# Seven block products for eight in the spatial product of an attention, MoE and gMLP kernel

## The chip, the cores and the metric

The kernel runs on one core of a Trainium2 chip. The metric is the device time of one execution in microseconds. The engines are TensorE (PE, with its weight loads shown as PEld), VectorE (DVE), ScalarE (ACT), GpSimd (POOL) and SyncE (SP), which here issues all transfers.

## What is computed

Three layers follow each other over 4 batches of 1088 tokens: a linear attention, a channel mix (the "MoE" layer) and a gated MLP with a spatial product. The change lies in the last one. Cut to what matters:

```python
def _moe2_ref(x, w_in, w_spatial, b_spatial, w_out):
    h = np.maximum(x @ w_in, 0.0)
    u, v = h[..., :512], h[..., 512:]
    v_n = (v - mean(v)) / np.sqrt(var(v) + 1e-06)
    v_s = np.einsum('ts,bsd->btd', w_spatial, v_n) + b_spatial[None, :, None]
    return ((u * v_s) @ w_out)
```

The spatial product takes, for each batch, the 1088 x 1088 matrix `w_spatial` times the normalised v of 1088 tokens x 512 features. All is float32. To hold precision at TensorE's fast rate, each operand is split into a high and a low part (H and L, `float32r`), and a product is three matmuls: L*H, H*H, H*L (`mm3`, L109 to 112).

## The kernel before

Tokens stand in three chunks `CH` of 384, 384 and 320 target tokens (c = 0, 1, 2). Source tokens stand in eight blocks of 128 (k = 0 to 7) and a tail of 64. The 512 features of v stand in four blocks of 128 (d = 0 to 3).

The first part (up to about 185 us) runs attention and the channel mix for all batches. Its plan gives each piece of work a step g (`plan`, `todo`); in it the weights of the spatial product are loaded and split (`wstep`, `wload`, `wconv`, L410 to 429), and four units of batch 0's gated MLP are put in early.

The second part goes over the batches. A unit is one pair (d, c): `spatial` (L487) makes the up-projection u of its feature block into bank 3 (`mm3`, then a relu by ScalarE, L503), adds eight blocks times three matmuls into one accumulator bank (L506), adds two tail matmuls with the bias (L511, L512), multiplies u by the accumulator on VectorE (L516), and splits that product (copy on ScalarE L519, subtract on VectorE L520). The product with `w_out` is left to a closure (`tail`, L522) that a later unit runs after its fourth block (`gout`, L507); on the fourth feature block its bank is copied and stored (L526, L527). A unit is so 24 + 2 + 3 + 3 = 32 matmuls, 12 units a batch. The very last unit ends in `finish` (L531): two halves on VectorE, each followed by a float32 matmul, a copy and the store.

The v of batch b+1 is made during batch b: `v_tile` (L444) does three matmuls of 512 columns into banks 6 and 7, a relu (L450), mean and variance on VectorE (L454, L455), the inverse root on GpSimd (L456, L457) and the scaling on VectorE (L458), into the tile `VR`, which stays in SBUF. `normalise` (L463) splits it per feature block: copies of 128x512 on ScalarE, subtracts on GpSimd (`low`, L118), and the tail's operands T1 and T2.

SBUF tiles have one buffer per tag and PSUM has eight banks with a tag each, so a new tile of a tag waits until the old one has been read. The order of the instructions on each engine is not the order of the text: a scheduler lays it out when the program is built, with modelled times (`schedule_with_timeline_sim=True`, L815).

Of the kernel before, what the change touches and what calls it, by code (L numbers as in the profile page):

```python
# [8 lines left out]
F32 = mybir.dt.float32  # L9
# [3 lines left out]
ALU = mybir.AluOpType  # L13
# [45 lines left out]
W1G = 69  # L59
W1N = 8  # L60
ORD0 = ((0, 0), (1, 0), (0, 1), (1, 1), (2, 0), (3, 0), (2, 1), (3, 1), (0, 2), (1, 2), (2, 2), (3, 2))
R0 = (1, 5)
R1 = 5
VW = NH * (HD + 1)


@with_exitstack
def attn_moe_gmlp(ctx: ExitStack, tc: tile.TileContext, qT, kT, va, st, wk, wv, wr, win, wout,
# [3 lines left out]

    pool = ctx.enter_context(tc.tile_pool(name="sb", bufs=1))
    pp = ctx.enter_context(tc.tile_pool(name="ps", bufs=1, space=PSUM))

    uid = [0]

# [15 lines left out]
    def m(i):  # L93
        return f"m{i}"
# [11 lines left out]
    ebias = sb("ebias", [128, 1])  # L106
    warm = sb("warm", [128, 1])

    def mm3(out_ap, lH, lL, rH, rL, first, last, late=1):  # L109
        parts = [(lL, rH), (lH, rH), (lH, rL)]  # L110
        for n, (l, r) in enumerate(parts if late else parts[::-1]):
            TE.matmul(out_ap, lhsT=l, rhs=r, start=first and n == 0, stop=last and n == 2)  # L112

    def copy(dst, src):
        return SE.activation(out=dst, in_=src, func=AF.Copy)  # L115
# [274 lines left out]
            VE.tensor_tensor(out=xTs[b][:, o:o + n], in0=vvs.pop(i), in1=sgs.pop(i), op=ALU.mult)  # L390


    wt, xsp, vnt = {}, {}, {}

    WTAGS = (8, 9, 10, 11, 12, 13, 14, 15, 16, 17, 0, 1, 2, 3, 4, 5, 6, 7)

# [44 lines left out]
            low(VE, xL[:, S:], x3, xH[:, S:])  # L441
        xsp[b] = (xH, xL)

    def v_tile(b, j):  # L444
        xH, xL = xsp[b]
        v = VR[:, j]
        pv = bank(rot(6, 7))
# [10 lines left out]
        VE.tensor_scalar(out=v, in0=v, scalar1=mv[:, 0:1], scalar2=rs, op0=ALU.subtract, op1=ALU.mult)  # L458

    GRP = {0: ((0, 8),), 1: ((0, 8),), 2: ((0, 3), (3, 3), (6, 2)), 3: ((0, 8),)}  # L460
    TAGS = {0: (("n0H", "n0L"),), 1: (("n1H", "n1L"),), 2: ((m(8), m(9)), (m(10), m(11)), (m(12), m(13))), 3: (("k0", "k1"),)}

    def normalise(b, d):  # L463
        cs = slice(128 * d, 128 * d + 128)
        Hs, Ls = [], []
        for (j0, n), (tH, tL) in zip(GRP[d], TAGS[d]):
            H, L = sb(tH, [128, n, 128], F32R), sb(tL, [128, n, 128], F32R)
            for j in range(0, n, 4):
                e = min(n, j + 4)
# [13 lines left out]
        vnt[b, d] = (Hs, Ls, T1, T2)  # L483

    po, gout, seen = {}, [], {}

    def spatial(b, d, c, fill, early=False):  # L487
# [17 lines left out]
        for k in range(NK):  # L505
            mm3(acc, Hs[k], Ls[k], *wtile(k, c), k == 0, False, 0)  # L506
            if k == 3 and gout:  # L507
                gout.pop()()
# [4 lines left out]
        if (b, rank, c) == (B - 1, ND, NCH - 1):  # L513
            finish(b, d, c, acc, u)
            return
        VE.tensor_tensor(out=u, in0=acc, in1=u, op=ALU.mult)  # L516
        gH = sb("xrH" if early else rot(m(2), m(3)), [128, n], F32R)
        gL = sb("xrL" if early else rot(m(4), m(5)), [128, n], F32R)
        copy(gH, u)  # L519
        low(VE, gL, u, gH)  # L520

        def tail():  # L522
            mm3(po[c], woH[:, ds], woL[:, ds], gH, gL, rank == 1, rank == ND)
            if rank == ND:
# [6 lines left out]
    def finish(b, d, c, acc, u):  # L531
        o, n = CH[c]
        while gout:
            gout.pop()()
        ob = sb(rot(m(6), m(7)), [128, n])
        step = n // 2
        parts = [slice(x, x + step) for x in range(0, n, step)]
        for cs in parts:
            VE.tensor_tensor(out=u[:, cs], in0=acc[:, cs], in1=u[:, cs], op=ALU.mult)
            TE.matmul(po[c][:, cs], lhsT=wo_last, rhs=u[:, cs], start=False, stop=cs is parts[-1])  # L540
        copy(ob, po[c])
        nc.sync.dma_start(out=out[:, b * S + o:b * S + o + n], in_=ob)


    rawS = sb(m(9), [128, 16, 2], I32)
# [180 lines left out]
        for fn in todo.pop(g, ()):  # L726
            fn()
    assert not todo
    wo_last = sb(m(14), [128, 128])
    ds = slice(DG - 128, DG)  # L730
# [4 lines left out]
    for b in range(B):  # L735
        if b + 1 < B:
            xsplit(b + 1)
        order = ORD0 if b == 0 else [divmod(u, NCH) for u in range(ND * NCH)]
        for u, (d, c) in enumerate(order):
            if b == 0 and u < EARLY:  # L740
                continue
            fill = {}

            def add(k, fn, *a):
                fill.setdefault(k, []).append(lambda: fn(*a))

            if b == 0:
                for k in range(WB[u] if u < len(WB) else 0):
                    add(k, wstep)
            elif u == 0:  # L750
                add(0, normalise, b, ND - 1)
            if b + 1 < B:
                vt = {2: (0, 1), 3: (2, 3), 4: (4, 5), 5: (6, 7), 6: (8,) * (b % 2)}.get(u - (VD0 if b == 0 else 0), ())
                for n, j in enumerate(vt):
                    add(2 + 3 * n, v_tile, b + 1, j)
                nd = {NB0: 0, NB0 + 1: 1, NB0 + 2: 2} if b == 0 else {7: 0, 8: 1, 10: 2}
                if u in nd:
                    add(0, normalise, b + 1, nd[u])
            spatial(b, d, c, fill)
    assert wi[0] >= len(worder) and not pending_raw  # L760
    while gout:
        gout.pop()()


_INS = ["qT", "kT", "va", "st", "wk", "wv", "wr", "win", "wout", "wT", "wtail", "btail", "mu", "ident", "msk"]
# [53 lines left out]
```

## Time and profile before

| what | value |
|---|---|
| median of 3 runs | 469.09 us (468.9 to 469.63) |
| the profiled execution's own time | 468.87 us |
| its span in the trace | 467.1 us |
| TensorE busy | 454.6 us, 97% |
| VectorE / ScalarE / GpSimd busy | 50% / 52% / 41% |

The span is what the trace covers; the execution's own time has some 1.8 us around it. A row of a group of instructions names the line, the engine, the operation, what is written and read (tile names without numbers; `p` is a PSUM bank, `w` the weights' tiles, `m` scratch), how often, the busy time and the mean of one. A timeline row has start and duration in us; consecutive equal instructions are merged (x20), and their durations overlap where the engine is pipelined.

### The profile page before, as it was taken

To read this page: it belongs to the slowest core of one execution; us is meant where nothing else is said; L and a number is where in the kernel's file an instruction comes from. 1 tells how busy PE (TensorE), PEld (TensorE's weight loads), DVE (VectorE), ACT (ScalarE), POOL (GpSimd) and SP (SyncE) were. 2 spreads that over 40 slices of the span, in tenths; PEclk is the share of its full clock that TensorE was granted. 3 is DMA by queue.
4 is the path that set the end of the run, shared out by engine and by line. 5 is a ranking of instruction groups with operands and counts; after the bars stand their busy time and mean duration, and the time that the engine had idled before them with its cause. 6 is when DMAs were issued, how large, how long until landed. Compare 5 with 4: busy or idle time off the path is not lost.

```text
span 467.1 us, 7331 instructions
## 1 busy us (share of the span) xinstructions
PE 454.6 (97%) x2757; PEld 432.7 (93%) x2757; DVE 234.4 (50%) x430; ACT 240.6 (52%) x567; POOL 191.7 (41%) x248
## 2 busy tenths in 40 slices
PE   8978999999999998999999999999999999999997
PEld 8967998989998887999999999999999999999996
DVE  4598768768446796337653435521335421212121
ACT  2585768888776987685327423441433441312111
POOL 2566546486544898455217313440213430200000
PEclk9999999999999999999999999999999999999999
DMA  7972100011000110122000000000100000000001
GB/s 221 359 241 93 49 0 2 17 34 52 27 1 1 42 60 20 34 81 64 1 17 18 15 1 1 0 2 0 50 1 1 0 1 17 32 1 0 2 0 48
DMA packets 12227, 18.77 MB, mean 40 GB/s; under 512 B 1760, under 2 KB 10784, under 8 KB 12192
## 3 DMA queue, kind: packets, MB, share of 16 engines
q1 hardware_dynamic: 12192, 18.31, 12.2%
q8 instruction: 21, 0.34, 0.3%
q14 instruction: 14, 0.11, 0.1%
HBM read 16.08 MB, written 2.23 MB: 39 GB/s over the span
## 4 chain that ended last, share of the span: by engine, by line
PE 78%; DVE 8%; POOL 5%; DMA 3%; ACT 2%; issue 2%; SPq 1%; ACTq 0%; POOLq 0%; DVEq 0%
PE p L112 64%; PE p L386 4%; DVE w L118 2%; POOL m L343 2%; PE p L258 2%; PE p L511 2%; PE p L512 2%; PE p L220 2%; DVE w L128 1%; DMA w<-in_wk_dram 1%; PE p L189 1%; DMA w<-in_qT_dram 1%; PE p L241 1%; DVE mx L298 1%; ACT m L340 1%
## 5 line engine op out<-in xcount | busy, mean ns | idle before, releaser
L516 DVE TENSOR_TENSOR m<-p,m 128x384 f32<-128x384 f32 (+1 forms) x43 | 22.9, 533 | 93.2 <-PE p L512 89.0
L112 PE MATMUL p<-m,k 128*128 128x384 f32 (+1 forms) x288 | 65.8, 348 | 2.7 <-POOL k L133 1.6
L503 ACT ACTIVATE m<-p 128x384 f32<-128x384 f32 (+1 forms) x44 | 20.7, 470 | 75.6 <-PE p L112 73.6
L343 POOL TENSOR_TENSOR m<-m 128x384 f32<-128x384 f32 (+1 forms) x48 | 42.9, 898 | 38.2 <-ACT m L340 32.6
L112 PEld LDWEIGHTS p<-m,k 128*128 128x128 f32 x288 | 48.3, 188 | 6.4 <-POOL k L133 1.8
L112 PE MATMUL p<-w,k 128*128 128x384 f32 (+1 forms) x288 | 52.0, 327 | 0.0
L112 PE MATMUL p<-w,m 128*128 128x384 f32 (+1 forms) x288 | 51.7, 327 | 0.0
L112 PE MATMUL p<-w,n1H 128*128 128x384 f32 (+1 forms) x192 | 48.4, 328 | 0.2 <-DVE x L516 0.2
L112 PEld LDWEIGHTS p<-w,m 128*128 128x128 f32 x288 | 48.1, 188 | 0.4
L112 PEld LDWEIGHTS p<-w,k 128*128 128x128 f32 x288 | 48.0, 188 | 0.3
L340 ACT ACTIVATE m<-p 128x384 f32<-128x384 f32 (+1 forms) x96 | 42.5, 471 | 11.0 <-PE p L112 8.3
L112 PE MATMUL p<-w,n0H 128*128 128x384 f32 (+1 forms) x192 | 48.0, 329 | 0.0
L118 DVE TENSOR_TENSOR w<-m,w 128x384 fp32r<-128x384 f32 (+1 forms) x44 | 33.4, 765 | 28.5 <-POOL m L343 17.0
L118 DVE TENSOR_TENSOR m<-m,m 128x384 fp32r<-128x384 f32 (+1 forms) x47 | 28.9, 616 | 35.5 <-ACT m L115 30.0
L456 POOL TENSOR_SCALAR rs<-mv 128x1 f32<-128x1 f32 x34 | 9.4, 277 | 66.6 <-DVE mv L455 64.1
L450 ACT ACTIVATE VR<-p 128x512 f32<-128x512 f32 x34 | 20.3, 601 | 31.2 <-PE p L112 31.1
L112 PEld LDWEIGHTS p<-w,n1H 128*128 128x128 f32 x192 | 34.3, 188 | 1.5 <-DVE x L516 0.5
L112 PEld LDWEIGHTS p<-w,n0H 128*128 128x128 f32 x192 | 34.1, 188 | 0.8
L386 PE MATMUL p<-w,wvT 128*128 128x384 f32 (+1 forms) x88 | 34.3, 471 | 0.0
L112 PE MATMUL p<-w,n0L 128*128 128x384 f32 (+1 forms) x96 | 31.8, 331 | 0.9 <-POOL n0L L118 0.9
L112 PE MATMUL p<-w,n1L 128*128 128x384 f32 (+1 forms) x96 | 31.7, 330 | 0.0
L454 DVE BATCH_NORM_STATS2 bn<-VR 128x6 f32<-128x512 f32 x34 | 23.3, 688 | 13.8 <-ACT VR L450 13.8
(193 smaller groups left out, 1031.2 us busy)
## 6 DMA issues: line engine op xcount, KB each, us to landing
st<-in_wT_dram SPq DMA_DIRECT2D x16, 192.0 KB, 2.4
w<-in_kT_dram SPq DMA_DIRECT2D x8, 192.0 KB, 4.8
w<-in_qT_dram SPq DMA_DIRECT2D x8, 192.0 KB, 4.7
out_dram<-m SPq DMA_DIRECT2D x8, 192.0 KB, 1.9
st<-in_wT_dram SPq DMA_DIRECT2D x8, 160.0 KB, 2.2
xs0H<-in_va_dram SPq DMA_DIRECT2D x2, 528.0 KB, 5.2
xs0L<-in_va_dram SPq DMA_DIRECT2D x2, 528.0 KB, 6.2
w<-in_wk_dram SPq DMA_DIRECT2D x2, 512.0 KB, 6.8
```

The source lines that it names most:

```text
L112: TE.matmul(out_ap, lhsT=l, rhs=r, start=first and n == 0, stop=last and n == 2)
L118: return eng.tensor_tensor(out=L, in0=src, in1=H.bitcast(F32), op=ALU.subtract)
L220: TE.matmul(kv[:, w * g:w * g + w], lhsT=kp, rhs=vt if wide else vt[:, VP * g:VP * g + VP], start=(t == 0), stop=(t == NT - 1))
L258: nd_pe[0] = TE.matmul(o.rearrange("p h c -> p (h c)"), lhsT=qt[g][:, cut(c, t)], rhs=kb[:, g], start=not wide or g == 0, stop=not wide or ...
L340: SE.activation(out=r, in_=hk, func=AF.Relu)
L343: anchor[2] = GE.tensor_tensor(out=sq, in0=r, in1=r, op=ALU.mult)
L386: TE.matmul(vvs[i], lhsT=wvT[:, f // 2], rhs=hls.pop(g), start=f == 0, stop=f == NF - 1)
L450: SE.activation(out=v, in_=pv, func=AF.Relu)
L454: VE.bn_stats(out=bn, in_=v)
L456: GE.tensor_scalar(out=rs, in0=mv[:, 1:2], scalar1=1e-6, scalar2=None, op0=ALU.add)
L503: SE.activation(out=u, in_=pu, func=AF.Relu)
L516: VE.tensor_tensor(out=u, in0=acc, in1=u, op=ALU.mult)
```

## The change

For batches 1 to 3 units are replaced by groups. A group (b, p) takes two feature blocks d = p and e = p + 2, and all three chunks. For chunks 0 and 1 the source blocks are cut into two halves of four. That makes a 2 x 2 block product (features by source halves, source halves by chunks), which Strassen's scheme (in Winograd's form) does in seven products of four blocks each, in place of eight. Chunk 2 is done as before, with eight blocks per output.

The scheme needs sums of blocks on both sides. Sums of the weights (sets 1 to 4 in `ctile`, and the tail's set 5) are made once, during units 4 to 11 of batch 0, from weights loaded again: for each block k of a half, two VectorE operations for sets 1 and 3 and three for sets 2 and 4, and per set a copy on ScalarE and a subtract on GpSimd (table `W2`). Sums of v are made per group by `build`: four VectorE operations of 128x512, and for each of the eight sets a copy of 128x512 on ScalarE and a subtract on GpSimd.

v of batches 1 to 3 no longer stays in `VR`: `v_tile` writes it to DRAM, and `quad_load` reads a quarter (four blocks of one feature block, 512 bytes a row) back for each of the four operands of a group. Banks: 0 is X, 1 is Y, 6 is Z and chunk 2's accumulator, 3 and 7 rotate between up-projections and V tiles, 2, 4 and 5 hold the output products. In chunks 0 and 1 the relu of u is no longer ScalarE's: one VectorE instruction takes the maximum of the bank and zero and multiplies by the joined product (`gated_out`).

Cut to its core:

```diff
+W2 = {4: ((6, "fl", 2),), 5: ((1, "fs", 2), (1, "fl", 3)), 6: ((1, "fs", 3), (2, "fl", 0)),
+      7: ((1, "fs", 0), (2, "fl", 1)), 8: ((1, "fs", 1), (4, "sl", 2), (4, "sl", 0)), 9: ((1, "ss", 2), (4, "ss", 0), (7, "sl", 1)),
+      10: ((4, "ss", 1), (7, "sl", 3)), 11: ((4, "ss", 3),)}
+BUILD = (11, 12, 22, 21, 2, 1, 3, 4)
+RING = ("n1H", "n1L", "k0", "k1")
...
-    def v_tile(b, j):
+    def v_tile(b, j, banks=(6, 7)):
...
+        if b and j < NK:
...
+            nc.sync.dma_start(out=vdram[b][:, j], in_=v)
...
+    def parts(n, k, src):
+        H, L = ctile(n, k)
+        copy(H, src)
+        low(GE, L, src, H)
+
+    def first_sums(k):
+        r11, r12, r22 = raws.pop(k)
+        tt(VE, r11, r12, r11, ALU.subtract)
+        parts(1, k, r11)
+        tt(VE, r22, r22, r12, ALU.subtract)
+        parts(3, k, r22)
...
+    def build(b, p, i):
+        n = BUILD[i]
+        A = {x: quad.get((b, p, x)) for x in (11, 12, 21, 22)}
+        if n == 2:
+            tt(VE, A[22], A[21], A[22], ALU.add)
+            tt(VE, A[21], A[11], A[21], ALU.subtract)
+            tt(VE, A[11], A[22], A[11], ALU.subtract)
+        if n == 4:
+            tt(VE, A[12], A[12], A[11], ALU.subtract)
...
+        copy(t[:, 0], src)
+        low(GE, t[:, 1], src, t[:, 0])
...
+        def gated_out(pu, C, d, c):
+            VE.scalar_tensor_tensor(out=C, in0=pu, scalar=0.0, in1=C, op0=ALU.max, op1=ALU.mult)
+            put_out(b, d, c, C)
...
+        d, e = p, p + 2
+        X = bank(0)[:, :CMAX]
+        prod(X, 11, 11, True)
+        a = snap(X)
+        flush()
+        u = pre(d, 2, True)
+        acc = bank(6)[:, :CH[2][1]]
+        plain(acc, 11, True)
+        flush()
+        yield
+        Y = bank(1)[:, :CMAX]
+        prod(Y, 12, 21, True)
+        tmm(Y, d, wtile(NK, 0))
+        pu = pre(d, 0)
+        gated_out(pu, join(Y, a), d, 0)
+        plain(acc, 12, False)
+        tmm(acc, d, wtile(NK, 2))
+        tt(VE, u, acc, u, ALU.mult)
+        put_out(b, d, 2, u)
+        yield
+        Y = bank(1)[:, :CMAX]
+        prod(Y, 22, 4, True)
...
+        yield
+        prod(X, 2, 2, False)
+        u2 = snap(X)
+        flush()
+        yield
+        Z = bank(6)[:, :CMAX]
+        prod(Z, 1, 1, True)
+        yield
+        prod(X, 3, 3, False)
+        tmm(X, e, wtile(NK, 1))
+        u3 = snap(X)
+        pu = pre(e, 1)
+        c22 = sb(rot(m(8), m(9), m(10), m(11)), [128, CMAX])
+        gated_out(pu, join(Z, u3, c22), e, 1)
+        pu = pre(e, 0)
+        gated_out(pu, join(Y, u3), e, 0)
+        yield
+        prod(Z, 4, 22, False)
+        tmm(Z, d, wtile(NK, 1))
+        if last_group:
+            while gout:
+                flush()
+            pu = pre(d, 1)
+            ob = sb(rot(m(6), m(7)), [128, CMAX])
+            for h in range(2):
+                cs = slice(CMAX // 2 * h, CMAX // 2 * h + CMAX // 2)
+                tt(VE, u2[:, cs], Z[:, cs], u2[:, cs], ALU.add)
+                VE.scalar_tensor_tensor(out=u2[:, cs], in0=pu[:, cs], scalar=0.0, in1=u2[:, cs], op0=ALU.max, op1=ALU.mult)
+                TE.matmul(po[1][:, cs], lhsT=wo_last, rhs=u2[:, cs], start=False, stop=h == 1)
...
+        else:
+            flush()
+            pu = pre(d, 1)
+            gated_out(pu, join(Z, u2), d, 1)
...
+        for st, _ in enumerate(group(b, p)):
+            if st < 4:
+                build(b, p, st + 4)
+            elif nxt:
+                build(*nxt, st - 4)
+            if nxt:
+                if st in (1, 2):
+                    quad_load(*nxt, (11, 12)[st - 1])
+                if st in (3, 4):
+                    quad_load(*nxt, (22, 21)[st - 3])
+                if st in (5, 6):
+                    tails(nxt[0], nxt[1] + 2 * (st - 5), vtail[:, 0])
+            if b + 1 < B:
+                if p == 0:
+                    v_tile(b + 1, st, (3, 7))
+                elif st == 0 and b % 2:
+                    v_tile(b + 1, NK, (3, 7))
```

In it `prod(acc, a, w, first)` is four blocks of `mm3` with v's set a and the weights' set w, `plain` the same with chunk 2's weights, `tmm` the two tail matmuls, `pre` the three matmuls of an up-projection, `snap` ScalarE's copy of a bank to SBUF, `join` a VectorE add of a bank and such a copy, `flush` the next output product that waits, and `put_out` the split of a gated product. `finish` is gone.

## Rows read from the trace of the kernel before

**Rows 1.** The page's head and busy times by engine, whole span.
```profile
span 467.1 us, 7331 instructions
...
PE 454.6 (97%) x2757; PEld 432.7 (93%) x2757; DVE 234.4 (50%) x430; ACT 240.6 (52%) x567; POOL 191.7 (41%) x248
```
**Rows 2.** Busy time per stretch: batch 0's second part, batches 1 to 3.
```profile
core 0: us, PE busy (x) PEld busy (x) DVE busy (x) ACT busy (x) POOL busy (x), PEclk, DMA share, GB/s
215.00:262.00 47.00, 47.00 (x283) 45.95 (x282) 24.32 (x49) 22.89 (x51) 19.03 (x30) 1.00 0.06 18
262.00:462.00 200.00, 200.00 (x1191) 197.74 (x1190) 64.19 (x125) 60.05 (x134) 40.39 (x62) 1.00 0.02 8
```
**Rows 3.** Waits of TensorE from 185 us on, all of them.
```profile
engine line waited for: us in total, times, longest us
PE p L112 <- DVE x L516: 0.2, 1, 0.2
```
**Rows 4.** Timeline of TensorE: 20 matmuls and the next one.
```profile
431.69 3.65 PE L112 MATMUL p<-w,m 128*128 128x384 f32 x20
435.18 0.31 PE L112 MATMUL p<-m,woL 128*128 128x320 f32 x1
```
**Rows 5.** Timeline of the last 5 us, from the last tail matmuls.
```profile
462.10 0.31 PE L511 MATMUL p<-w,T 128*128 128x320 f32 x1
...
462.24 0.31 PE L512 MATMUL p<-w,wrH 128*128 128x320 f32 x1
...
462.59 0.56 DVE L539 TENSOR_TENSOR m<-p,m 128x160 f32<-128x160 f32 x2 [2.29 <-PE p L512]
...
464.33 0.33 SPq L542 DMA_DIRECT2D out_dram<-m  x1
```
**Rows 6.** Timeline: a last matmul and its reader.
```profile
441.90 0.33 PE L512 MATMUL p<-w,T 128*128 128x384 f32 x1
...
442.28 0.56 DVE L516 TENSOR_TENSOR m<-p,m 128x384 f32<-128x384 f32 x1 [3.40 <-PE p L512]
```
**Rows 7.** Instruction groups from 262 to 462 us, other engines.
```profile
L516 DVE TENSOR_TENSOR m<-p,m 128x384 f32<-128x384 f32 (+1 forms) x35 | 18.8, 536 | 85.6 <-PE p L512 81.4 <-ACT m L115 4.1
...
L503 ACT ACTIVATE m<-p 128x384 f32<-128x384 f32 (+1 forms) x36 | 17.0, 472 | 70.3 <-PE p L112 68.3 <-DVE m L516 1.9
...
L454 DVE BATCH_NORM_STATS2 bn<-VR 128x6 f32<-128x512 f32 x17 | 11.8, 692 | 10.0 <-ACT VR L450 10.0
...
L450 ACT ACTIVATE VR<-p 128x512 f32<-128x512 f32 x17 | 10.2, 600 | 22.9 <-PE p L112 22.9
L457 POOL TENSOR_TENSOR rs<-rs,half 128x1 f32<-128x1 f32 x17 | 9.6, 563 | 1.3
L458 DVE TENSOR_SCALAR VR<-VR,mv,rs 128x512 f32<-128x512 f32 x17 | 9.3, 546 | 11.2 <-POOL rs L457 11.2
...
L118 POOL TENSOR_TENSOR n1L<-VR,n1H 128x512 fp32r<-128x512 f32 x4 | 5.2, 1294 | 3.0 <-ACT n1H L115 3.0
...
L115 ACT ACTIVATE n1H<-VR 128x512 fp32r<-128x512 f32 x4 | 2.5, 628 | 1.3 <-PE p L112 1.3
```
**Rows 8.** Timeline of TensorE: output matmuls between two tail matmuls.
```profile
457.26 0.34 PE L511 MATMUL p<-w,T 128*128 128x384 f32 x1
457.44 0.34 PE L112 MATMUL p<-m,woL 128*128 128x384 f32 x1
457.61 0.34 PE L112 MATMUL p<-m,woH 128*128 128x384 f32 x1
457.79 0.34 PE L512 MATMUL p<-w,wrH 128*128 128x384 f32 x1
```
**Rows 9.** Line L118 over the span: duration ns min/median/max.
```profile
L118 DVE TENSOR_TENSOR w<-m,w x44: 478/558/1620, 27.9 to 190.2; 128x384 fp32r<-128x384 f32 x32, 128x320 fp32r<-128x320 f32 x12
L118 POOL TENSOR_TENSOR w<-st,w x15: 877/1015/1338, 89.4 to 217.1; 128x384 fp32r<-128x384 f32 x11, 128x320 fp32r<-128x320 f32 x4
```
**Rows 10.** Transfers by issue: KB each, median us to landing.
```profile
st<-in_wT_dram SPq DMA_DIRECT2D x16, 192.0 KB, 2.4
...
out_dram<-m SPq DMA_DIRECT2D x8, 192.0 KB, 1.9
```
**Rows 11.** Transfer queue: packets, MB, share of 16 engines' time.
```profile
q1 hardware_dynamic: 12192, 18.31, 12.2%
```
**Rows 12.** Timeline of TensorE: the last V tile of batch 1.
```profile
239.02 0.39 PE L112 MATMUL p<-winL,xs1H 128*128 128x512 f32 x1
```

More of the change, by code (lines that the diff above doesn't have):

```diff
@@ L107, in attn_moe_gmlp, with mm3 @@
     warm = sb("warm", [128, 1])
-    def mm3(out_ap, lH, lL, rH, rL, first, last, late=1):
+    def mm3(out_ap, lH, lL, rH, rL, first, last, late=1, skip=False):
         parts = [(lL, rH), (lH, rH), (lH, rL)]
         for n, (l, r) in enumerate(parts if late else parts[::-1]):
-            TE.matmul(out_ap, lhsT=l, rhs=r, start=first and n == 0, stop=last and n == 2)
+            TE.matmul(out_ap, lhsT=l, rhs=r, start=first and n == 0, stop=last and n == 2, skip_group_check=skip)
     def copy(dst, src):
@@ L529, in spatial @@
         gout.append(tail)
[L531 to L542, printed above, removed]
+    ct = {}
@@ new lines, in tt, with stage, first_load @@
+    def tt(eng, o, a, b_, op):
+        return eng.tensor_tensor(out=o, in0=a, in1=b_, op=op)
+    raws = {}
+    def stage(j):
+        return VR[:, j, :CMAX]
+    def first_load(k):
+        raws[k] = [stage(j) for j in rot(*FSET)]
+        for x, n in zip(raws[k], (11, 12, 22)):
+            wraw(x, n, k)
+    def parts(n, k, src):
[8 more added lines that the diff above has]
+        parts(3, k, r22)
@@ new lines, in second_load, with second_sums, tail_sums @@
+    def second_load(k):
+        raws[k] = [stage(j) for j in SSET[k]]
+        for x, n in zip(raws[k], (11, 21)):
+            wraw(x, n, k)
+    def second_sums(k):
+        a, c = raws.pop(k)
+        H, L = [x.bitcast(F32) for x in ctile(3, k)]
+        tt(VE, a, a, H, ALU.add)
+        tt(VE, a, a, L, ALU.add)
+        tt(VE, c, c, a, ALU.subtract)
+        parts(2, k, a)
+        parts(4, k, c)
+    def tail_sums():
+        H, L = ctile(5, NK)
+        x, y = sb(m(10), [128, CMAX]), sb(m(11), [128, CMAX])
+        nc.sync.dma_start(out=x, in_=btail[:, :CMAX])
+        nc.sync.dma_start(out=y, in_=btail[:, CMAX:2 * CMAX])
+        tt(VE, x, x, y, ALU.subtract)
+        parts(5, NK, x)
+        VE.tensor_copy(L[64:65], H[64:65].bitcast(F32))
+        copy(H[64:128], H[0:64].bitcast(F32))
@@ L760, in attn_moe_gmlp, with add @@
-    assert wi[0] >= len(worder) and not pending_raw
+    vtail = sb("wvT", [128, 1, DG])
+    GE.tensor_copy(vtail[:, 0], VR[:, NK])
+    xsplit(1)
+    for u, (d, c) in enumerate(ORD0):
+        if u < EARLY:
+            continue
+        fill = {}
+        def add(k, fn, *a):
+            fill.setdefault(k, []).append(lambda: fn(*a))
+        for k in range(WB[u] if u < len(WB) else 0):
+            add(k, wstep)
+        for n, j in enumerate({4: (0, 1), 5: (2, 3), 6: (4, 5), 7: (6, 7)}.get(u, ())):
+            add(2 + 3 * n, v_tile, 1, j)
+        for k, fn, *a in W2.get(u, ()):
+            add(k, {"fl": first_load, "fs": first_sums, "sl": second_load, "ss": second_sums}[fn], *a)
+        if u == 9:
+            for n in (11, 12):
+                add(2, quad_load, 1, 0, n)
+        if u == 11:
+            for n in (22, 21):
+                add(0, quad_load, 1, 0, n)
+        if u == 10:
+            add(2, tails, 1, 0, vtail[:, 0])
+            add(1, build, 1, 0, 0)
+        if u == 11:
+            add(1, build, 1, 0, 1)
+        spatial(0, d, c, fill)
@@ new lines, in attn_moe_gmlp @@
+    assert wi[0] >= len(worder) and not pending_raw
+    groups = [(b, p) for b in range(1, B) for p in range(2)]
+    for gi, (b, p) in enumerate(groups):
+        nxt = groups[gi + 1] if gi + 1 < len(groups) else None
+        if gi == 0:
+            tail_sums()
+            build(1, 0, 2)
+            tails(1, 2, vtail[:, 0])
+            build(1, 0, 3)
+        if p == 0 and b + 1 < B:
+            xsplit(b + 1)
+        for st, _ in enumerate(group(b, p)):
[10 more added lines that the diff above has]
+                    tails(nxt[0], nxt[1] + 2 * (st - 5), vtail[:, 0])
+            if b + 1 < B:
+                if p == 0:
+                    v_tile(b + 1, st, (3, 7))
+                elif st == 0 and b % 2:
+                    v_tile(b + 1, NK, (3, 7))
```

151 lines of the change are left out of this document (109 added, 42 removed).

## The prediction

> **What bounds the kernel now.** I read the busy shares first [rows 1]: TensorE 97%, the others half or less. A share over the whole span can hide a stage with another limit, so I then took the stretches that the change touches [rows 2]. In batch 0's second part (215 to 262 us) and in batches 1 to 3 (262 to 462 us) TensorE is busy in every microsecond at a granted clock of 1.00 (2.4 GHz), while VectorE, ScalarE and GpSimd are busy 32%, 30% and 20% of the latter. Busy matmuls can overlap and so hide idle time; the view of waits excludes that: after 185 us TensorE waits once, for 0.2 us [rows 3]. So from 185 us to the end the time is the number of matmuls times their spacing. One matmul of 384 columns lasts 0.34 us, but matmuls are pipelined, so that is not their spacing: 20 of them begin at 431.69 and the next matmul at 435.18 [rows 4], which is 3.49 / 20 = 175 ns.
>
> **The products removed: -12.6 us.** Two halves of the eight source-token blocks, two feature blocks (d, d+2) and two chunks of targets took 4 outputs x 8 blocks x 3 = 96 matmuls. Seven half-length products take 7 x 4 x 3 = 84. All other matmuls (the two tail matmuls per output, the up-projections, the output products, chunk 2) keep their number. Twelve fewer in each of 6 groups is 72, all of 384 columns: 72 x 0.175 = 12.6 us. Nothing else fills TensorE here, so all of it is on the path.
> The Trainium skill's page "TensorE: Matmul & The Clock Gate", section "Back-to-back issue gap", gives columns / 2.4 + 2.5 ns for a warm matmul, 162.5 ns here; by it the saving is 11.7 us and the total 0.9 us higher. The trace has 175, and I keep that.
>
> **The end: +0.6 us.** Before, the last two tail matmuls start at 462.10 and 462.24 and VectorE's halves start at 462.59; three output matmuls run beside them; the span ends at 467.1, 4.86 us after 462.24 [rows 1, 5]. The last group instead flushes two output products and makes an up-projection behind its last product: 9 matmuls, 1.58 us, before the gate can read the up-projection. VectorE's first half then starts some 1.95 us after the last tail matmul began in place of 0.35, so the tail is 1.6 us longer; but 9 - 3 = 6 matmuls (1.05 us) of the count have moved into it. Net 0.55 us. The join of the halves runs beside those matmuls and is free; that cover goes if the scheduler puts the flushes earlier, but so does the 0.55.
>
> **Hand-overs of PSUM banks: +3.0 us (0 to 6).** Now every product is 12 matmuls (2.1 us) and products share banks: X is read and added to again, Y and Z as well. I went through each place where TensorE writes a bank that another engine has just read, or needs a weight just built. All but one have a product of 2.1 us or more between; the shortest of these is the output product flushed after product M2 (it needs a multiply, a copy and a subtract, some 2.2 us against 2.6 of cover). The one that is short is Z before its second product: the tail matmul of M3 ends in X, ScalarE copies X out, VectorE adds that to Z, and only then may TensorE add to Z. In rows: 0.38 from the start of a last matmul to its reader (441.90 to 442.28) [rows 6], 0.47 for the copy, 0.56 for the add [rows 7], and 0.1 for two signals, in all 1.51 us. Behind the tail matmul stand two up-projections, 6 matmuls; with its own slot 7 x 0.175 = 1.22 us. So 0.3 us is bare. In two groups (pass 0 of batches 1 and 2) a V tile stands there too, whose bank is held until the gate has read the up-projection, 0.6 us more: 0.9. 4 x 0.3 + 2 x 0.9 = 3.0 us. The low bound is 0: the instruction order is made by a scheduler at build time, and before it puts matmuls of one chain between those of another (two output matmuls between the tail matmuls, 457.26 to 457.79 [rows 8]), so it may put the next group's first product there. The high bound is twice it, 6.0, if a VectorE instruction of 0.5 us stands ahead of the add in each group. I take 3.0, since no row shows this gap filled.
>
> **Other engines in batches 1 to 3: 0.** VectorE gets 24 adds of 128x512 (no row; by 0.56 for 384 columns about 0.75, 18 us) and 24 joins (13.4 us). ScalarE gets 24 more copies of 128x512 at 0.63 and 18 snapshots for 24 activations less, about +12 us; GpSimd 24 more subtracts at 1.29, 31 us [rows 7]. With what they do now, 64, 60 and 40 us of 200 [rows 2], none passes 52% of the 187 us that remain. Each set is built two stages or more (at least 24 matmuls, 4.2 us) before its product; that is the cover.
>
> **Batch 0: +0 (0 to 4).** The sums of weights add 20 VectorE adds (11 us), 16 copies (8 us) and 16 GpSimd subtracts at 1.02 (16 us) [rows 9] to 24, 23 and 19 us of 47 [rows 2]; some 8 us of GpSimd work (batch 1's splits, four of 1.29 us and three shorter ones) moves later, less 2.6 for two new sets. TensorE hides it while each unit's subtract comes within a unit (32 matmuls, 5.6 us). The sums themselves are needed from the fifth stage of the first group, 17 us after batch 0.
>
> **Transfers: 0.** 20 weight blocks, 2 tail rows, 24 writes of V and 24 reads are issued on SP's queue, 70 x 0.33 us [rows 5] over 250 us. Weight loads land in 2.4 us, stores in 1.9 [rows 10]. The reads come in 512-byte pieces, 512 packets; 12,192 packets now take 12.2% of 16 engines' 467 us [rows 11], 75 ns each, so one takes about 512 / 16 x 75 ns = 2.4 us. The chain from the last V tile of batch 1 to a weight is some 10 us (0.6 relu, 1.7 statistics and GpSimd, 0.55 scaling, 1.9 + 2.4 transfers, 1.9 to build, and signals); that tile's matmuls begin at 239.02 [rows 12], and its first use lies past 262. SP's queue holds output stores behind a read that waits for its buffer; nobody waits for those but the output copy two units later.
>
> **Sum.** -12.6 + 0.55 + 3.0 = -9.05. The profiled execution's own time is 468.87, so 459.8; the median of the runs is 0.22 higher, hence **460.0**.
>
> **Rivals.**
> *All covered* (18%): the scheduler fills the bare place, -12.05, 457.0 us; without the tail's cost 456.5. For it: one short wait in 280 us before. Against: the order is laid out with modelled times, and the new chain is serial.
> *The joins queue up* (21%): VectorE works in order, and next to the joins stand statistics (0.69), scaling that waits for GpSimd, and 0.75 us adds. If in each group one such instruction with its wait, 0.9 us, stands ahead of the join, 6 x 0.9 = 5.4 on top: 465.4 us, the case spanning 462 to 468. For it: the fixed order and two more dependent steps; against: VectorE is about half busy.
> *No change* (4%): the hand-overs give back 12.05 / 6 = 2.0 us a group, nearly a whole product; then 469. This is also what the profile would show if the added products were not the ones left out: the matmul count tells.
> *Batch 0 dams up, slower* (7%): VectorE and GpSimd slow each other. The subtract of row L118 takes 558 ns at the median and up to 1,620, GpSimd's 1,015 and up to 1,338 [rows 9]. At a stretched 1.4 and 1.34 us the additions alone are 20 x 1.4 + 16 x 1.34 = 49 us; with GpSimd's other 11 to 14 (19 less 8, and the two sets) and VectorE's other two-input subtracts, a dozen of 0.56, this passes the 47 us by some 20, each unit's subtract waits in that queue, and TensorE with it: about 480 us. It decides against the change where the overrun passes 9 us, that is, where the additions take over 38 us of shared time; at median rates they are 20 x 0.56 + 16 x 1.02 = 27 us.
> The Trainium skill's page "SBUF — State Buffer", section "Who interferes with whom", says that a VectorE instruction with two SBUF inputs and a GpSimd one that reads SBUF exclude each other for a whole instruction; by that the two add up rather than overlap. The long maxima agree with it.
>
> **How the numbers follow.** The forecast has 50%, its own range 458.5 to 462. The range takes in full cover (456.5) and most of the queued joins: 456.5 to 467.5; outside lie no change, slower and a sliver of the third case, some 13%. A measurement of this kernel tells about 0.2%, 0.9 us. Faster 50 + 18 + 21 = 89%, same 4%, slower 7%.
>
> **What would show it.** 72 matmuls fewer and the spacing still 175 ns; TensorE waiting for a VectorE add once a group, 0.3 to 0.9 us, 3 us in all; batch 0's second part no longer than 47 to 48 us; at the end about 6.5 us from the last product's tail matmul to the end. Wrong would be waits of TensorE on GpSimd or DMA in batch 0, waits at more than one place of a group, a changed first part (before 185 us), or a granted clock under 1.00.

## The result and the profile after

The changed kernel takes 471.84 us (median of 11 runs, 470.84 to 474.71), the kernel before 469.09 beside it (11 runs): a ratio of 1.006, 95% interval 1.0043 to 1.0078. It is 0.6% slower; the forecast was 460.0 (456.5 to 467.5). The medians below leave out one execution each of e1, e2 and e5, which ran 5% to 90% longer than the others of the same kernel.

The page's head and busy times of the changed kernel, as [rows 1]:
```profile
span 472.9 us, 7556 instructions
...
PE 447.5 (95%) x2685; PEld 421.6 (89%) x2685; DVE 288.1 (61%) x501; ACT 260.6 (55%) x600; POOL 244.7 (52%) x287
```
72 matmuls are gone (2757 to 2685), as forecast, but TensorE is no longer busy throughout. All of its waits from 185 us on, in place of the single one of [rows 3]:
```profile
PE p L124 <- ACT m L127: 5.8, 5, 2.0
PE p L124 <- DVE m L577: 2.4, 3, 1.2
PE p L124 <- DVE m L130: 1.5, 2, 1.2
PE p L124 <- DVE x L402: 1.4, 1, 1.4
PE p L124 <- ACT m L519: 0.5, 1, 0.5
PE p L124 <- ACT m L352: 0.4, 1, 0.4
PE p L124 <- DVE x L529: 0.2, 1, 0.2
```
To compare stretch by stretch I cut both traces at the same matmuls: the second tail matmul of unit (1, 1), that of batch 0's last unit, and the last one of all. The two middle stretches in the changed kernel, then a part of the first of them:
```profile
core 0: us, PE busy (x) PEld busy (x) DVE busy (x) ACT busy (x) POOL busy (x), PEclk, DMA share, GB/s
215.30:271.26 55.96, 49.59 (x278) 46.57 (x278) 39.31 (x70) 25.80 (x59) 34.60 (x42) 0.97 0.48 151
271.26:466.81 195.55, 190.18 (x1126) 185.60 (x1125) 103.04 (x176) 77.22 (x159) 78.84 (x90) 1.00 0.17 54
256.40:259.80 3.40, 3.40 (x13) 3.40 (x14) 0.83 (x2) 1.18 (x3) 1.60 (x2) 0.51 0.73 199
```
The two stretches before:
```profile
213.83:260.18 46.35, 46.35 (x278) 45.30 (x278) 25.00 (x49) 21.61 (x48) 18.03 (x29) 1.00 0.06 19
260.18:462.24 202.06, 202.06 (x1203) 199.80 (x1202) 64.68 (x126) 61.80 (x138) 41.83 (x63) 1.00 0.02 8
```

| stretch, us | before | after | difference | forecast |
|---|---|---|---|---|
| start to unit (1, 1) | 213.83 | 215.30 | +1.5 | 0 |
| batch 0's second part | 46.35 | 55.96 | +9.6 | 0 (to 4) |
| batches 1 to 3, to the last tail matmul | 202.06 | 195.55 | -6.5 | -10.65 |
| from there to the end | 4.86 | 6.09 | +1.2 | +1.6 |
| span | 467.1 | 472.9 | +5.8 | -9.05 |

(-10.65 is the forecast's -12.6, less 1.05 for the six matmuls that it put into the tail, plus 3.0 for the hand-overs.) Batch 0's second part has the same 278 matmuls and lost most. The profiled execution took 474.71 us, 2.9 over the median, so a usual run loses less than this table shows; the stretch at 0.51 of full clock (256.4 to 259.8 us) is part of it.

**Inside batch 0.** VectorE's timeline there; the columns are start, duration, engine, line, operation, and in brackets the idle time before it and what ended that:
```profile
235.82 0.56 DVE L577 TENSOR_TENSOR VR<-VR,t 128x384 f32<-128x384 f32 x1 [1.85 <-DMA VR<-in_wT_dram]
...
236.90 0.54 DVE L577 TENSOR_TENSOR VR<-VR,t 128x384 f32<-128x384 f32 x1
237.36 0.54 DVE L470 TENSOR_SCALAR VR<-VR,mv,rs 128x512 f32<-128x512 f32 x1
238.18 1.31 DVE L577 TENSOR_TENSOR VR<-VR,x 128x384 f32<-128x384 f32 x1 [0.28 <-DMA VR<-in_wT_dram]
...
239.51 0.52 DVE L529 TENSOR_TENSOR m<-p,m 128x384 f32<-128x384 f32 x1
```
And TensorE's, at the same place:
```profile
237.56 1.04 PE L124 MATMUL p<-w,m 128*128 128x384 f32 x5
240.63 0.44 PE L124 MATMUL p<-m,woL 128*128 128x384 f32 x1 [2.03 <-ACT m L127]
```
The last tail matmul of this unit began at 231.60 us. Its multiply (L529) runs at 239.51, behind three adds of the weight sums (L577): the first waited 1.85 us for a reloaded block, the last 0.28 us and then took 1.31. Copy and output matmul follow the multiply, and TensorE stands 2.0 us. The wait is put down to ScalarE's copy, the last link; the late ones are the adds ahead of the multiply, two links back.

The block is late because SyncE's queue, which issues the reloads (L574), works in order too:
```profile
225.57 0.54 SPq L574 DMA_DIRECT2D VR<-in_wT_dram  x1
231.59 0.33 SPq L474 DMA_DIRECT2D vd<-VR  x1
232.06 2.63 SPq L574 DMA_DIRECT2D VR<-in_wT_dram  x3
```
From 226.1 to 231.6 us it stands at a store of V (L474), whose scaling VectorE finishes only then; three reloads stand behind that store, and the add of 235.82 starts when the first of them has landed. SyncE's waits of this kind from 210 to 272 us are 14.4 us in all:
```profile
SPq L474 <- DVE VR L470: 14.4, 6, 5.4
```
So two queues hold each other up: reloads wait for VectorE's scaling, and VectorE's gate (multiply, and later the subtract) waits behind adds for the reloads. No run issued the reloads ahead of the stores, so what this order alone costs is open.

### The profile page after: what moved, and what is told of

Same layout as the page of the kernel before. It is cut to its first block, busy times and chain, and to the rows that moved or that the text cites. A ratio compares the mean times of both kernels' runs of the same rounds, so it can differ in the third digit from the quotient of the medians.

```text
span 472.9 us, 7556 instructions
## 1 busy us (share of the span) xinstructions
PE 447.5 (95%) x2685; PEld 421.6 (89%) x2685; DVE 288.1 (61%) x501; ACT 260.6 (55%) x600; POOL 244.7 (52%) x287
## 4 chain that ended last, share of the span: by engine, by line
PE 59%; DVE 16%; POOL 10%; DMA 5%; issue 4%; ACT 4%; SPq 1%; POOLq 0%; ACTq 0%; DVEq 0%
PE p L124 47%; DVE VR L470 4%; PE p L398 4%; DVE w L130 2%; DMA VR<-in_wT_dram 2%; POOL m L355 2%; PE p L270 2%; DVE bn L466 2%; POOL rs L469 2%; PE p L232 2%; DMA w<-in_wk_dram 2%; DVE w L140 1%; POOL w L130 1%; PE p L201 1%; DMA w<-in_qT_dram 1%
## 5 line engine op out<-in xcount | busy, mean ns | idle before, releaser
L130 POOL TENSOR_TENSOR k<-VR,k 128x512 fp32r<-128x512 f32 x26 | 33.9, 1305 | 47.4 <-ACT k L127 35.4
L577 DVE TENSOR_TENSOR m<-p,m 128x384 f32<-128x384 f32 (+2 forms) x37 | 19.2, 520 | 61.0 <-PE p L676 34.1
L352 ACT ACTIVATE m<-p 128x384 f32<-128x384 f32 (+1 forms) x96 | 42.4, 470 | 11.1 <-PE p L124 8.3
L127 ACT ACTIVATE m<-m 128x384 fp32r<-128x384 f32 (+2 forms) x45 | 22.7, 504 | 38.1 <-DVE m L689 27.0
L470 DVE TENSOR_SCALAR VR<-VR,mv,rs 128x512 f32<-128x512 f32 x33 | 31.6, 963 | 15.5 <-POOL rs L469 15.2
L127 ACT ACTIVATE k<-VR 128x512 fp32r<-128x512 f32 x26 | 16.2, 629 | 36.5 <-PE p L124 28.4
L124 PEld LDWEIGHTS p<-w,n1L 128*128 128x128 f32 x168 | 29.2, 192 | 0.3
L466 DVE BATCH_NORM_STATS2 bn<-VR 128x6 f32<-128x512 f32 x33 | 22.5, 686 | 11.0 <-ACT VR L462 10.9
L124 PE MATMUL p<-m,woH 128*128 128x384 f32 (+1 forms) x86 | 26.6, 332 | 1.5 <-DVE m L130 1.5
L124 PE MATMUL p<-w,xs1H 128*128 128x384 f32 (+1 forms) x88 | 25.1, 339 | 2.9 <-DVE w L130 2.9
L130 POOL TENSOR_TENSOR n1H<-VR,n1H 128x512 fp32r<-128x512 f32 x12 | 15.5, 1292 | 23.1 <-ACT n1H L127 18.8
```

The costliest lines, as they stand in the source:

```text
L130: return eng.tensor_tensor(out=L, in0=src, in1=H.bitcast(F32), op=ALU.subtract)
L352: SE.activation(out=r, in_=hk, func=AF.Relu)
L577: return eng.tensor_tensor(out=o, in0=a, in1=b_, op=op)
```

## The experiments

Theories. **W**: batch 0's loss is VectorE's queue standing behind adds that wait for late reloads. **C**: it is the added work itself, VectorE and GpSimd slowing each other. **J**: the waits in batches 1 to 3 come from what stands ahead of the join on VectorE, or ahead of the snapshot on ScalarE.

**e1_no_sums**: no reloads and no sums; the products read resident weight blocks, so batches 1 to 3 compute something else.
```
-        if n == 4:
-            return wtile(k, 1)
+        if n in (1, 2, 3, 4):
+            return wtile(*{1: (k, 0), 2: (k + HALF, 1), 3: (k + HALF, 0), 4: (k, 1)}[n])
...
-        for k, fn, *a in W2.get(u, ()):
+        for k, fn, *a in ():
```


> The sums of weights and their reloads are left out; the seven products take plain weights in their place (so sets 1 to 4 are not the scheme's). Everything else stays: 84 products a group, V through DRAM, the same hand-overs. In the changed kernel batch 0's second part ends 9.6 us later than before relative to its start. Theory 1, that the work added to batch 0 is the loss: that part is back within 1 us of the 46.3 us it took before (213.83 to 260.18), and the median falls by 8 to 10 us to some 463 us. Rival, that V's trip through DRAM and the three V slots delay batch 0: the part stays over 50 us and the median over 467.

**e3_reloads_only**: the reloads stay, first_sums and second_sums return at once.

> The 20 reloads are issued as in the change, but no sum is made of them (sets 1 to 4 are plain weights). If the transfers alone were the loss (SP's queue in order, V's stores behind the reloads, V slots), batch 0's second part would stay over 51 us and the median over 467. Theories W and C both say that transfers alone cost little: the part within 2 us of the run without sums and reloads, median 463 to 465.

**e2_sums_of_resident**: the sums stay, made of the high parts of resident blocks; no reloads.
```
-        tt(VE, r11, r12, r11, ALU.subtract)
+        tt(VE, r11, h12, h11, ALU.subtract)
```


> The sums are made by the same VectorE, ScalarE and GpSimd instructions, but from the weights' high parts that lie in SBUF, with no reload (20 transfers of 192 KB less; the low parts are left out of the sums). Theory W, that VectorE's queue stands still at adds whose blocks land late: batch 0's second part falls by 5 us or more, median 465 to 467. Theory C, that VectorE and GpSimd slow each other and the amount of work is the loss: it falls by less than 2.5 us, median over 469.5, and adds beside a GpSimd subtract still take 1.0 us or more instead of 0.56.

Measured: e1 465.12 us (ratio to before 0.9908, 0.9894 to 0.9922), e3 465.17 (0.9914, 0.9902 to 0.9927), e2 468.83 (0.999, 0.9981 to 0.9999). e1 falls by 6.7 us, not by the 8 to 10 that I had taken from the profiled execution. Batch 0's second part is 46.4 us in e1, 46.1 in e3 and 50.2 in e2. The stretch of [rows 2] in e3, then in e2:
```profile
215.00:262.00 47.00, 47.00 (x283) 45.80 (x282) 25.08 (x52) 19.88 (x45) 14.88 (x27) 1.00 0.53 171
```
```profile
215.00:262.00 47.00, 44.43 (x257) 41.90 (x256) 37.75 (x65) 23.73 (x53) 34.60 (x41) 1.00 0.32 103
```
The transfers alone cost nothing, at 171 GB/s in place of 18. The sums alone cost 3.8 us of the part (50.2 against 46.4; 3.7 by the medians of e2 and e1): that is C. What is left needs both, adds that wait for what is reloaded (W): 471.84 - 468.83 = 3.0 us by the medians, 5.8 in the profiled execution, with its stretch at half clock. So neither theory alone is enough: the part falls by what W asked for (5 us or more), the median lies between the two forecasts. The trip of V through memory is in all three and costs nothing in this part.

**e7_no_gpsimd_subtracts**: the sums' 16 GpSimd subtracts become ScalarE copies, so the sums' low parts are other numbers.
```
-        low(GE, L, src, H)
+        copy(L, src)
```


> The changed kernel (its own order) in which the 16 GpSimd subtracts of the weight sums, about 1.0 us each, are 16 ScalarE copies; the low parts of the sums then hold the whole sums, so the output of batches 1 to 3 is not the reference's. It measures what GpSimd's share of the sums costs by itself. Theory C (GpSimd's subtracts slow VectorE's two-input instructions beside them, 3.8 us of the 9.6 that batch 0's second part lost): the part falls from 56 to about 52 us and the time from 471.8 to about 468. Theory W alone (VectorE's adds wait for transfers, and GpSimd has nothing to do with it): within 1 us of the changed kernel. More than 5 us less would say that the waits for transfers arise only because the slowed adds release the staging buffers late.

Measured 469.87 us (1.0009, 0.9998 to 1.0019), second part 49.2 us. VectorE's adds there, and what they waited for:
```profile
L577 DVE TENSOR_TENSOR VR<-VR x11: 541/551/801, 217.4 to 259.0; 128x384 f32<-128x384 f32 x11
...
  DMA VR<-in_wT_dram: 7.8, 7
```
The part is 6.7 us shorter than in the changed kernel's profile, of which 1.7 return behind it; by the medians, which leave out that profile's 2.9 us, the kernel is 2.0 us faster. That lies between the theories: C's 3.8 us are not all GpSimd's. Nor do the shares simply add. In e2, seven adds that read two resident blocks have a median of 1281 ns, beside GpSimd; in the changed kernel, whose adds wait for reloads, the ten of the largest group have 546 ns (both for L577 from 215 to 262 us). e2's 3.7 us is what the sums cost where nothing waits, not a part of the changed kernel's time that can be pointed at. The adds still wait 7.8 us for reloads (4.5 us in the changed kernel in the same window), so these waits don't come from slowed adds that free the staging buffers late.

**e4_order**: in each group the two up-projections go behind X's last tail matmul, and the next group's copies and tails behind the snapshot.
```
-        pu = pre(e, 1)
+        pu = behind([x_last], pre, e, 1)
...
-                build(*nxt, st - 4)
+                behind(snapped if st == 6 else [], build, *nxt, st - 4)
```


> Only the order is changed: the two up-projections are queued behind X's last tail matmul of product M3 (the scheduler had put them ahead of it), and the copies of the next set and tail that ScalarE does there are queued behind the snapshot of X. Theory O, that the hand-over of Z is bare because its cover was moved ahead of it and ScalarE's copies stand before the snapshot: the six gaps of TensorE, 0.8 to 1.3 us each (6.2 in all) fall to 0.3 or less in the four groups without V tiles, 3.5 to 4.5 us, median 467.3 to 468.5. Rival J, that the join waits behind VectorE's scaling: the gaps at M4 of pass 0 of batches 1 and 2 (1.0 and 0.5) stay, and if all are of that kind the median falls by less than 1.5 us.

Measured 466.73 us (0.9946, 0.9932 to 0.996). That is 5.1 us less than the changed kernel, more than the 3.5 to 4.5 that I expected. A hand-over of the changed kernel, with the first matmul of its two up-projections:
```profile
328.23 0.34 PE L124 MATMUL p<-xs1H,winL 128*128 128x384 f32 x1
...
334.07 0.34 PE L676 MATMUL p<-w,wrH 128*128 128x384 f32 x1
...
334.14 0.63 ACT L127 ACTIVATE k<-VR 128x512 fp32r<-128x512 f32 x1 [1.35 <-issue]
334.68 0.29 ACT L127 ACTIVATE T<-wvT 64x128 fp32r<-64x128 f32 x1
...
334.88 0.47 ACT L127 ACTIVATE m<-p 128x384 f32<-128x384 f32 x1
...
335.40 0.79 PE L124 MATMUL p<-w,n1H 128*128 128x384 f32 x3 [0.99 <-ACT m L127]
```
The same place in e4_order:
```profile
331.22 0.34 PE L676 MATMUL p<-w,wrH 128*128 128x384 f32 x1
...
331.39 0.34 PE L124 MATMUL p<-xs1H,winL 128*128 128x384 f32 x1
...
331.59 0.49 ACT L127 ACTIVATE m<-p 128x384 f32<-128x384 f32 x1 [0.43 <-PE p L676]
...
332.44 1.38 PE L124 MATMUL p<-w,n1H 128*128 128x384 f32 x7
```
In the changed kernel the instruction order had put the up-projections 5.8 us ahead of the tail matmul, so nothing stood between it and the next group's first product, which writes the same bank; and the snapshot that frees the bank stood behind a 0.63 us copy for a later product. In e4_order six matmuls cover a snapshot that starts at once. Four waits of 0.8 to 1.2 us are gone; two, of 0.9 and 0.7 us (0.8 and 0.4 in the changed kernel), stay in the groups that also make V tiles. The two halves of the edit were not tried apart.

**e8_join_first** (with e5's edit, below): the scaling of one V tile, and its store, go behind the join.
```
+                    if held:
+                        behind(joined, held.pop())
+                    f = v_tile(b + 1, st, (3, 7), st == 5)
```


> e5_late_weight with one edit in the groups that also make a V tile in every stage: the scaling of the V tile of the sixth stage, and its store, are queued behind the join that reads Z, instead of ahead of it. Theory J (in these two groups the join stands behind a scaling that waits for GpSimd, and TensorE waits 1.0 and 0.9 us at 301.5 and 368.2 us): both waits fall to 0.3 us or less, and the time falls by 1.0 to 1.4 us, to about 464.5. Rival (the join is late because of the chain copy, add, matmul itself; 0.6 us of bank wait): the waits stay above 0.6 us and the time falls by under 0.5 us.

Measured 464.15 us (0.9896, 0.9882 to 0.9909). Both waits are gone; TensorE is busy throughout batches 1 to 3:
```profile
267.54:456.25 188.71, 188.59 (x1126) 185.81 (x1125) 103.05 (x175) 76.94 (x159) 79.54 (x90) 1.00 0.17 56
```
J holds. The gain is larger than the 1.0 to 1.4 us expected: 2.3 to 2.9 us on e5's two runs, and 2.2 us in this stretch (190.86 in e5b). The stretch is 6.8 us shorter than in the changed kernel (195.55), and 13.35 shorter than before: 77 matmuls fewer, which are 81 of 384 columns less and 4 of 320 more, 81 x 0.175 - 4 x 0.147 = 13.6.

**e5_late_weight** and **e5b_late_weight_again** (e4_order and this edit): the sum of the output weights is made in batch 0, not at 162 us.
```
-    GE.tensor_tensor(out=wo_last, ...)
...
+            behind([vt_copy], GE.tensor_tensor, wo_last, ...)
```


> The e4_order kernel with one more edit: the sum woH + woL (the weight of the last two matmuls, one GpSimd add of 0.62 us) is queued on GpSimd behind the copy of V's ninth tile, in batch 0's second part, instead of at build time wherever a buffer is free. In the changed kernel that add stands at 162.1 us between the two GpSimd steps (add, power) that a V tile's scaling waits for. Theory (the add delays the last V tile before the first tail matmul, and the rest of the first part is as before): the first tail matmul of unit (1,1) goes back from 214.6 to about 213.6 to 213.9 us, and the time falls by 0.7 to 1.2 us against e4_order (466.73), to about 465.7. Rival (the first part's extra 1.0 to 1.5 us is scatter from run to run, or comes from the new buffers' places): no change, 466.7.

> e5_late_weight once more, unchanged: it was to be 0.7 to 1.2 us faster than e4_order (466.73) and came out at 467.06, while two kernels that hold its edit (e6 and e8) have their first tail matmul of unit (1,1) at 214.0 us against 214.56 in e4_order. Theory (the edit gives back 0.6 us of the first part, and batch 0's second part took it away again, by 0.5 to 1 us more of waits there): unit (1,1) at 214.0 us, second part 55.5 us or longer, time 466.2 to 467.2. Rival (the edit gains nothing, and 214.0 belongs to the other edits): unit (1,1) at 214.5 or later.

GpSimd's timeline in the changed kernel:
```profile
161.45 0.59 POOL L468 TENSOR_SCALAR rs<-mv 128x1 f32<-128x1 f32 x1
...
162.13 0.62 POOL L953 TENSOR_TENSOR idn<-woH,woL 128x128 f32<-128x128 f32 x1
...
162.71 0.56 POOL L469 TENSOR_TENSOR rs<-rs,half 128x1 f32<-128x1 f32 x1
...
163.30 1.51 DVE L470 TENSOR_SCALAR VR<-VR,mv,rs 128x512 f32<-128x512 f32 x1 [0.87 <-POOL rs L469]
```
Measured 467.06 us (0.995, 0.9937 to 0.9963), and 466.46 again (0.9938, 0.9924 to 0.9951), against 466.73 (0.9946, 0.9932 to 0.996). In e5b's trace unit (1, 1) is at 213.78, as before the change (213.83; e4_order 214.56), and the second part takes 53.9 us (e4_order's profile, which has the half clock, 55.0). That comparison alone is weak, since traces differ by up to 0.9 us from early on: the matmul that begins at 161.69 us before the change, just ahead of this place, begins between 161.43 and 162.29 in the others. Counted from that matmul, unit (1, 1) comes 52.1 us later before the change, 53.1 in each of the six traces with the early add (the changed kernel, e1, e2, e3, e4, e7), and 52.1 to 52.5 in the five with the late one (e5b, e6, e8, e9, e10). So the add costs 1.0 us, and the edit gives back 0.6 to all of it; the other 0.5 us of the table's +1.5 is such scatter, as the rival said. The forecast of a longer second part was wrong; and of the 1.0 us at most a few tenths are left at the end, which is below what the runs can tell.

**e6_sums_behind** (e5 and this edit): the sums' adds go behind the subtract that ends the previous unit's gate (its multiply, copy and subtract).
```
-            add(k, {"fl": first_load, "fs": first_sums, ...}[fn], *a)
+            add(k, (lambda f, a: behind(gls[-1:], f, a)) if fn[1] == "s" else lambda f, a: f(a), f, *a)
```


> e5_late_weight with the weight sums' VectorE adds queued behind the subtract that ends the last unit's gate, so that a unit's multiply and subtract stand ahead of adds that wait for late reloads; everything else as there. Theory W (most of batch 0's extra 9 us is VectorE's queue standing behind adds that wait for transfers): batch 0's second part falls from 55 us to about 50, and the time to 460 to 462 us. Rival C (VectorE and GpSimd slow each other and simply have more to do; the order hardly matters): the part stays above 53 us and the time within 1.5 us of e5_late_weight. Between them, 462 to 464, if the waits only move to the next unit.

Measured 463.92 us (0.9882, 0.9869 to 0.9895):
```profile
214.00:260.13 46.13, 46.13 (x276) 44.97 (x276) 30.52 (x61) 22.37 (x49) 26.27 (x38) 1.00 0.51 163
```
The second part is 46.1 us, shorter than I expected, without one wait of TensorE, and 17 of the sums' 20 adds are made in it. But four waits came at 261 to 271 us (0.3, 1.7, 1.1 and 0.6 us), where batch 0's last two gates stand behind slowed adds and the split of batch 2's tokens. In all it gains 2.5 to 3.1 us on e5's two runs, close to W's 3.0; the time lies where I had put it if the waits only move.

**e9_both_orders** (e6 and e8 together) and **e10_split_behind** (e9, and the split behind the last gate):
```
-            xsplit(b + 1)
+            behind(gls[-1:] if gi == 0 else [], xsplit, b + 1)
```


> The edits of e6_sums_behind and of e8_join_first in one kernel. Theory (they cure waits at different places, so they add): batch 0's second part 46 us as in e6, no waits of TensorE at 297 and 364 us as in e8, time 1.5 to 2 us under e6_sums_behind, 461.9 to 462.4 us. What is left then are four waits at 261 to 271 us, 4.3 us in all in e6's trace, where the gates of batch 0's last two units stand behind the split of batch 2's tokens and behind slowed adds. Rival (the waits are one backlog of VectorE that only moves): within 0.7 us of e6_sums_behind.

> e9_both_orders with one more edit: the split of batch 2's tokens (four VectorE subtracts and their copies) is queued behind the subtract that ends batch 0's last gate. In e6's trace two of these subtracts stand ahead of the last gate, 2.1 and 2.8 us for the pair and the third, slowed by GpSimd. Theory (these 4.9 us are what makes the four waits at 261 to 271 us): the waits fall from 4.3 us to 1 or less and the time to 458 to 459.5 us. Rival (the adds of the weight sums are what stands ahead, and the split only shares the blame): the waits keep 2 us or more, 460 to 461.5 us.

Measured: e9 462.2 us (0.9855, 0.9838 to 0.9872), e10 460.95 (0.9825, 0.9811 to 0.9838). The edits of e6 and e8 add (1.7 us under e6). The split's own part in the waits is small: in e9 three are left there, 0.3, 1.7 and 0.4 us, and in e10 two, 0.4 and 1.7 us, where a gate stands behind adds stretched by GpSimd:
```profile
265.27 0.48 DVE L535 TENSOR_TENSOR m<-p,m 128x320 f32<-128x320 f32 x1
265.67 1.26 DVE L583 TENSOR_TENSOR VR<-VR,t 128x384 f32<-128x384 f32 x1
266.96 1.34 DVE L628 CAST m<-m 1x384 fp32r<-1x384 f32 x1
268.33 1.24 DVE L583 TENSOR_TENSOR VR<-VR 128x384 f32<-128x384 f32 x1
269.49 0.48 DVE L130 TENSOR_TENSOR m<-m,m 128x320 fp32r<-128x320 f32 x1
```
There the rival was right. Part of the 1.25 us between e9 and e10 may be the clock's: e9's trace has a stretch at half clock there (0.79 of full speed from 264 to 272 us), e10's has none. From batch 0's last unit to the last tail matmul e10 takes 192.1 us against e8's 188.7, and its second part 46.6 against the 46.35 of before: 3.6 us of the sums' cost are left. That is near C's 3.7, as if order had cured the waiting for reloads and the shared time of VectorE and GpSimd had only moved; no run has these orders without the sums, so this is likely, not shown.

e10_split_behind beats the kernel before by 1.75% and the changed one by 2.3%, with the same sums and products.

## Why the prediction was wrong

**The step that failed first: "Batch 0: +0 (0 to 4)."** It compared totals of busy time with 47 us, and noted that TensorE is covered "while each unit's subtract comes within a unit". It cost 9.6 us in the profiled execution and 6.7 by the medians (471.84 less e1's 465.12). Two things were missing. One is the waits for reloads, 3.0 us: the prediction noted that the sums are needed 17 us later and took that as slack, but an add on an engine that works in order holds up what is behind it from the moment it waits for its data. The other is what the sums cost even where nothing waits, 3.7 us in e2, which the forecast had in its bound of 4 and set to zero in the sum. The stretching of VectorE's and GpSimd's instructions beside each other is part of it: without GpSimd's subtracts, and with 16 more copies on ScalarE, e7 is 2.0 us faster. Of the 11.8 us between 460.0 and 471.84, batch 0 is 6.7, the hand-overs are 4.1 above their 3.0, the first part is 1.0, and the tail -0.4; 0.4 us are left unexplained.

**"Transfers: 0".** Right of bandwidth (e3), wrong of when a reload is issued. It looked at what stands behind a read in SyncE's queue and took it for output stores alone; reloads stand there too, behind V's stores, which wait for VectorE (14.4 us, above). Once issued, the reloads take a median of 2.9 us to landing (up to 4.1) in place of 2.4. VectorE's adds stood idle for them 9.3 us in all, in 8 waits.

**Hand-overs: 3.0 forecast, 7.1 measured** (the stretch's -6.5 less the -13.6 of its matmuls). The profile shows one wait a group, as forecast, but of 0.4 to 1.2 us, 5.3 in all. Three (0.8, 0.4 and 1.2 us) lie at the place that I named, Z's second product, behind VectorE's add. The other three (1.0, 1.1 and 0.8) lie at the next group's first product, which the scheduler put ahead of it and which waits for X's snapshot; this move I had taken for the low bound of 0. I worked out Z's chain as if the instructions ran as written, with six matmuls behind X's tail matmul; the scheduler moved those ahead of it and put ScalarE's copy for a later product before the snapshot. The text used the scheduler's freedom for the low bound alone; it works both ways. The 7.1 us are above the high bound of 6.0 by 1.1; e4 and e8 take nearly all of it away.

**First part: taken as unchanged, without a reason.** One GpSimd add of 0.62 us, which ran at 205.48 us before and is free to move since its tile changed to a buffer that is free early, went in between two steps that a V tile's scaling waits for. It costs 1.0 us, which the traces with e5's edit have back, wholly or for the greater part.

**Right:** the 72 matmuls and their 175 ns. In e8, where nothing else is in the way after batch 0, the count of matmuls times their spacing gives the stretch (13.35 us less than before, 13.6 by the count). The tail (+1.6 forecast, +1.2 measured) was right in kind:
```profile
466.81 0.33 PE L676 MATMUL p<-w,T 128*128 128x384 f32 x1
...
467.72 0.61 DVE L756 SCALAR_TENSOR_TENSOR m<-p,m 128x192 f32<-128x192 f32 x2
...
469.96 0.33 SPq L759 DMA_DIRECT2D out_dram<-m  x1
```
The gate starts 0.91 us after the tail matmul rather than 1.95, as two of the flushes run behind the up-projection, not ahead of it.

**The rivals.** *Batch 0 dams up* (7%) named the place and the sign. Its mechanism, VectorE and GpSimd slowing each other, is a part of the loss, between e7's 2.0 and e2's 3.7 of 6.7 us; the waits for reloads are not in it. Its price, some 20 us, was too high by far, and the point from which it was to decide (an overrun of 9 us) assumed that the rest would save 9, where the hand-overs had already taken 4 of that. 7% was too little for a part where TensorE's cover is one unit long. *The joins queue up* described the two waits that e8 removes.

That the same computation takes 460.95 us in e10_split_behind, near the forecast's 460.0, is luck: e10 has no wait left at the hand-overs, where the sum has 3.0 us, and 3.6 us of the sums' cost, where it has 0. Of the prediction's own signs of being wrong, three came: waits at more than one place, a changed first part, and a granted clock under 1.00.

## What to carry to other kernels

Work that is added to an engine "with room" can be free only where it stands behind everything urgent in that engine's queue until its data is there, and in e10 even that left 3.6 us: list, for each added instruction and each transfer, what stands behind it and what it waits for. Where a scheduler lays out the order from modelled times, read the order it made around the change (or fix it by hand) before counting on cover in the source's order; here five orders were worth 10.9 us, nearly as much as the 72 matmuls. A wait that the profile puts down to the last link (ScalarE's copy) is followed back to the first instruction that was late.

## What the hardware showed unexpectedly

TensorE's granted clock fell to its lower level after pauses in batch 0: 0.51 of full speed (1.2 GHz) from 256.4 to 259.8 us, in which matmuls of 320 columns begin 267 ns apart in place of 147:
```profile
256.39 0.67 PE L124 MATMUL p<-m,woH 128*128 128x384 f32 x1 [1.20 <-DVE m L130]
256.86 0.47 PE L124 MATMUL p<-w,n1L 128*128 128x320 f32 x1
257.13 0.73 PE L124 MATMUL p<-w,n1H 128*128 128x320 f32 x2
```
That is 120 ns on each of some 13 matmuls, 1.6 us on top of waits of 0.5 and 1.2 us just before. A longer wait of the same trace, 2.0 us up to 240.63, leaves the clock at 1.00 (236 to 246 us), and e10's has a wait of 1.7 us at 268 to 270 us and 1.00 from 268 to 276; so the length of one pause does not decide it; what does was not tried.

GpSimd stretches VectorE's scaling as well. In the changed kernel, beside a GpSimd subtract of 1.00 us that begins 0.07 earlier, one scaling takes 1.22 us; from 272 us on the mean of 16 is 1104 ns, against the 546 of 17 in [rows 7]. The Trainium skill's page "SBUF — State Buffer", section "Who interferes with whom", counts this operation among those that can take the port pair which VectorE shares with GpSimd; the trace agrees:
```profile
253.78 1.00 POOL L130 TENSOR_TENSOR w<-VR,w 128x384 fp32r<-128x384 f32 x1
```
```profile
253.85 1.22 DVE L470 TENSOR_SCALAR VR<-VR,mv,rs 128x512 f32<-128x512 f32 x1 [0.53 <-POOL rs L469]
```
Even an instruction on one partition is caught: the cast of 1x384 in e10's rows above took 1.34 us, while GpSimd subtracts from 264.89 to 268.08 us, against 0.35 in e6, where GpSimd is idle beside it.
